# A fifth stack buffer, later loads of the read-out, and maxima's rows made by ScalarE and VectorE

## The chip, the cores and the metric

The kernel runs on one core of a Trainium2 chip. Five engines work side by side: TensorE (PE in the profile; its weight loads are PEld), VectorE (DVE), ScalarE (ACT), GpSimd (POOL) and SyncE (SP), which here only issues DMAs. The metric is the device time of one execution in microseconds (us), the median of several runs; less is better.

## The reference

It is one transformer block on 2048 rows of 512 columns in float32. A condition vector gives six modulation rows; the first half is attention with a memory, the second a feed-forward layer of 1792 columns. What this case touches is the attention: 32 heads of 16 columns, four segments of 512 rows, causal softmax within each segment, and a read-out of the memory of the segments before.

```python
for s in range(N):                       # N = 4 segments of L = 512 rows
    qs, ks, vs = q[:, :, s], k[:, :, s], v[:, :, s]
    logits = jnp.einsum("bhqd,bhkd->bhqk", qs, ks) * scale + mask
    p = _softmax(logits, axis=-1)
    a_dot = jnp.einsum("bhqk,bhkd->bhqd", p, vs)
    pq = phi(qs)
    num = jnp.einsum("bhld,bhde->bhle", pq, M)
    den = jnp.einsum("bhld,bhd->bhl", pq, z)[..., None] + 1e-6
    o = g * (num / den) + (1.0 - g) * a_dot
    outs.append(o)
    M = M + jnp.einsum("bhld,bhle->bhde", phi(ks), vs)
    z = z + jnp.einsum("bhld->bhd", phi(ks))
```

## The kernel before

**Stages.** First the projections q, k, v and the memory read-out for all segments (to about 195 us), then the attention loop (195 to 510), then the feed-forward layer. Every float32 matrix is split into a high and a low part, so that a product is three matmuls.

**Head groups.** The loop runs over 32 groups Q, each of four heads of one segment (Q // 8 is the segment). The split q and k of a group lie in DRAM (QD, KD) and are loaded into a pair of SBUF tiles, the stacks `qst` and `kst`: `load_stacks` (L175) issues four DMAs of 192 KB. There are four pairs of stacks (`NK`, L165); group Q uses pair Q % 4. `new_stack` (L168) allocates a pair and fills rows with ones by ScalarE.

**Two passes per group.** The S pass (`s_unit`, L616) multiplies q by k (matmul L625), and VectorE takes the causal maximum of each row with one instruction (`masked_max`, L613). The maxima (tile `nm`) are turned into two further rows of the q stack: `m_rows` (L634) splits them into high and low parts on POOL (a copy, L638, and a subtraction, L639) into a tile `nmr`; `m_put` (L642) transposes them by a matmul (L644) and ScalarE copies the result to `ms`; `m_send` (L651) sends `ms` by two small DMAs (L654) into rows 48 and 49 of the stack. The T pass (`t_unit`, L674) multiplies k by q with these 50 rows (L686), so that the maximum is subtracted within the product, ScalarE takes the exponential (L689), POOL zeroes what lies above the diagonal (L671), and `pv_part` (L705) multiplies by v (L714). The S pass of a group runs two groups ahead of its T pass (`LEAD`), and six PSUM banks named `att` are shared by both.

**Read-out.** Two groups make a unit U. `pv_out` and `pv_store` (L731) write the result to DRAM (TD); `pv_in` (L734) loads it back in another layout as `dn` (the denominators) and `opk`, and `am_in` (L743) the memory's part `amB`. `den` (L754) inverts `dn` on VectorE, `den_store` (L764) writes it to DRAM (RD, L765), `rb_in` (L767) loads it back broadcast over the columns (`rbB`), `mix` (L771) multiplies and adds on POOL, and the output projection (`wo_part`, L796) follows.

**What sets the order.** It is written out by hand. `ORDER` (L26) is the pattern of one group: S and T units and slots c0 to c19. The table `PRM` (L28) gives each step its slot: `ap(pos, f, ...)` (L912) puts step f of a group at slot pos, where 20 slots are one group; so `'stacks': -59` puts the loads of group Q at 20 Q - 59, slot c1 of the group Q - 3. The loop at L997 walks through the pattern and issues what stands at each slot. All DMAs of the loop go through SyncE's queue, which works in the order of the program and waits at a DMA whose source is not ready.

## Time and profile before

| | |
|---|---|
| median of 3 runs | 822.83 us (821.05 to 827.29) |
| profiled execution | 823.3 us, span 821.6 us |
| PE busy | 796.4 us (97%) |
| DVE busy | 561.7 us (68%) |
| ACT busy | 453.0 us (55%) |
| POOL busy | 278.0 us (34%) |
| mean granted TensorE clock | 0.946 |
| bytes moved by DMA | 156.25 MB, 190 GB/s on average |

A row of the profile names the engine, the line of the kernel, the operation and the tiles (out<-in, buffer numbers left out). Idle time stands in brackets with what ended it: `[1.58 <-DMA qst<-QD]` is an idle time of 1.58 us that ended when the load of a q stack landed. The granted clock is the share of TensorE's full clock that the chip allowed in a stretch. Matmul ends are modelled, so a busy PE need not be one that works at its peak.

### The profile page before, as it was taken

The numbers are of one execution on the slowest core, as the hardware profiler recorded it, in microseconds if no ns is written. First come the engines' busy times: TensorE is split into PE (matmuls) and PEld (weight loads), VectorE is DVE, ScalarE is ACT, GpSimd is POOL, SyncE is SP. The second block draws the span as 40 slices with busy tenths as digits, with TensorE's granted clock in tenths as the row PEclk, the third lists the DMA queues.
The fourth block names the chain that finished last, engine by engine and source line by source line (L and its number), as shares of the span: only waits on it lengthen the run. The fifth ranks groups of instructions, "written<-read, shape, count | busy, mean of one in ns | idle before, by whom it ended". The sixth has DMA issues, their size and how long they took to land.

```text
span 821.6 us, 14382 instructions
## 1 busy us (share of the span) xinstructions
PE 796.4 (97%) x4532; PEld 550.8 (67%) x4532; DVE 561.7 (68%) x1624; ACT 453.0 (55%) x882; POOL 278.0 (34%) x503
## 2 busy tenths in 40 slices
PE   9999999999999999999898989999999999999998
PEld 4887877866444445454454545778888888888887
DVE  6766684578967857687785879978758864533423
ACT  4544444536867756576575857676845336653221
POOL 2205252302567544465486746034100403210000
PEclk9999999999968757799897999999999999999999
DMA  9759655493665564576676785467675635545443
GB/s 342 265 218 324 240 205 211 139 380 74 164 175 141 146 165 114 165 202 171 175 194 149 217 237 164 150 222 257 203 243 171 205 128 161 173 146 163 147 147 116
DMA packets 96564, 156.25 MB, mean 190 GB/s; under 512 B 15332, under 2 KB 31076, under 8 KB 96488
## 3 DMA queue, kind: packets, MB, share of 16 engines
q1 hardware_dynamic: 95624, 153.76, 60.2%
q10 hardware_dynamic: 864, 1.57, 0.5%
q8 instruction: 36, 0.59, 0.3%
q14 instruction: 40, 0.33, 0.1%
HBM read 93.95 MB, written 60.83 MB: 188 GB/s over the span
## 4 chain that ended last, share of the span: by engine, by line
PE 81%; DMA 9%; DVE 3%; ACT 2%; POOL 2%; SPq 1%; issue 1%; ACTq 0%; DVEq 0%; POOLq 0%
PE bx L1062 8%; PE pv L714 8%; PE att L686 7%; PE bx L1332 5%; PE att L625 5%; PE q L318 5%; PE by L1332 5%; PE bv L1332 5%; PE bv L1062 4%; PE k L318 4%; PE v L469 4%; PE mm L802 3%; DMA qst<-QD 3%; DMA qst<-ms 3%; PE spare L1332 2%; PE by L1062 2%
## 5 line engine op out<-in xcount | busy, mean ns | idle before, releaser
L613 DVE CUSTOM_DVE_ANT_0 dump<-att,maskb 128x512 bf16<-128x512 f32 (+3 forms) x512 | 223.1, 487 | 69.5 <-PE att L625 42.2
L686 PE MATMUL att<-qst,kst 50*128 50x512 f32 (+3 forms) x512 | 140.1, 403 | 6.7 <-DMA qst<-ms 4.1
L625 PE MATMUL att<-kst,qst 48*128 48x512 f32 (+3 forms) x512 | 132.0, 376 | 8.7 <-DMA qst<-QD 6.6
L686 PEld LDWEIGHTS att<-qst,kst 50*128 50x128 f32 x512 | 87.0, 211 | 67.0 <-DVE nm L613 47.4
L625 PEld LDWEIGHTS att<-kst,qst 48*128 48x128 f32 x512 | 85.5, 212 | 29.1 <-ACT ptc L689 7.7
L689 ACT ACTIVATE pta<-att 128x512 f32<-128x512 f32 x128 | 69.5, 597 | 39.4 <-PE att L686 36.3
L689 ACT ACTIVATE ptb<-att 128x384 f32<-128x384 f32 x128 | 63.3, 496 | 38.8 <-PE att L625 32.7
L846 POOL TENSOR_TENSOR wb<-wa 128x256 f32<-128x256 f32 x24 | 20.8, 865 | 152.1 <-DVE hr L867 69.0
L689 ACT ACTIVATE ptc<-att 128x384 f32<-128x384 f32 x128 | 57.0, 492 | 0.3 <-PE att L686 0.2
L671 POOL TENSOR_SCALAR_AFFINE_SELECT pta<-pta 128x256 f32<-128x256 f32 x64 | 26.8, 419 | 84.8 <-ACT pta L689 84.8
L138 DVE TENSOR_TENSOR gl<-s,gh 128x512 fp32r<-128x512 f32 x34 | 24.0, 706 | 42.4 <-ACT gh L135 42.4
L671 POOL TENSOR_SCALAR_AFFINE_SELECT ptc<-ptc 128x256 f32<-128x256 f32 x128 | 51.7, 414 | 1.7 <-ACT ptc L689 0.3
L135 ACT ACTIVATE gh<-s 128x512 fp32r<-128x512 f32 x34 | 21.3, 628 | 47.1 <-PE spare L1332 17.4
L671 POOL TENSOR_SCALAR_AFFINE_SELECT ptb<-ptb 128x256 f32<-128x256 f32 x64 | 26.4, 412 | 51.4 <-ACT ptb L689 51.3
L1067 ACT ACTIVATE s<-s,b1t 128x512 f32<-128x512 f32 x42 | 30.3, 721 | 21.7 <-DVE s L1071 21.6
L613 DVE DVE_READ_ACCUMULATOR2_ANT nm<- 128x1 f32 x512 | 42.2, 82 | 0.0
L1071 DVE TENSOR_TENSOR s<-bv,s 128x512 f32<-128x512 f32 x28 | 19.2, 687 | 30.1 <-PE bv L1062 20.7
L714 PE MATMUL pv<-pta,V 128*32 128x512 f32 x208 | 35.1, 754 | 0.0
L504 POOL TENSOR_SCALAR qp<-qp 128x512 f32<-128x512 f32 x12 | 18.5, 1541 | 42.2 <-ACT qp L499 42.2
L714 PE MATMUL pv<-ptc,V 128*32 128x256 f32 (+1 forms) x416 | 30.8, 372 | 0.0
L138 DVE TENSOR_TENSOR w1ml<-s,w1mh 128x512 fp32r<-128x512 f32 x18 | 13.0, 720 | 21.5 <-ACT w1mh L135 21.5
L802 PE MATMUL mm<-woh,oh 128*128 128x512 f32 x52 | 26.8, 516 | 0.0
(372 smaller groups left out, 2073.3 us busy)
## 6 DMA issues: line engine op xcount, KB each, us to landing
GD<-s SPq DMA_DIRECT2D x56, 256.0 KB
s<-GD SPq DMA_DIRECT2D x52, 256.0 KB
kst<-KD SPq DMA_DIRECT2D x64, 192.0 KB
qst<-QD SPq DMA_DIRECT2D x64, 192.0 KB
QD<-q SPq DMA_DIRECT2D x16, 512.0 KB
KD<-k SPq DMA_DIRECT2D x16, 512.0 KB
TD<-ts SPq DMA_DIRECT2D x32, 256.0 KB
xt<-X2D SPq DMA_DIRECT2D x28, 256.0 KB
```

The source lines that it names most:

```text
L138: lo_eng.tensor_tensor(out=lo, in0=src, in1=hi.bitcast(F32), op=ALU.subtract)
L318: pe.matmul(ps, a[:, k, 128 * g:128 * g + 128], b[k], start=(k == 0 and i == 0), stop=(k == KB - 1 and i == 2))
L469: pe.matmul(ps, a[k][:, 128 * b:128 * b + 128], w[:, k, :], start=(k == 0 and i == 0), stop=(k == KB - 1 and i == 2))
L613: v.tensor_tensor_reduce(out=dump[n_dump[0] % 2][:, :n], in0=src, in1=maskb[:, 512 - n:], scale=-1.0, scalar=-4 * NEG, op0=ALU.add, op1=AL ...
L625: pe.matmul(ps[:, o:o + n], q[:, 128 * i:128 * i + 128], k[:, :n], start=True, stop=True)
L671: pool.affine_select(out=t, in_=t, pattern=pattern, compare_op=ALU.is_ge, fill=0.0, base=0, channel_multiplier=-1)
L686: pe.matmul(ps[:, o:o + n], k[:, 128 * j:128 * j + 128], q[:, 128 * j:], start=True, stop=True)
L689: act.activation(pt[:, h, :], ps[:, :m], AF.Exp, scale=0.25)
L714: pe.matmul(ps[32 * c:32 * c + 32, lo:hi], V[4 * s + j][:, VW * hd:VW * hd + 32], pt[:, c // 2, lo - o:hi - o], start=start, stop=stop)
L802: pe.matmul(ps, a[:, 128 * b:128 * b + 128], w[:, g, :], start=(g == 0 and i == 0), stop=(g == 3 and i == 2))
L1062: pe.matmul(ps, a[:, i, k, :], b[k], start=start and k == 0 and c == 0, stop=k == 1 and c == 2, skip_group_check=not start)
L1332: pe.matmul(ps, a[:, c], w[:, lo:hi], start=(f == 0 and i == 0), stop=(last and i == 2))
```

## The change

There are four edits, made together.

1. **Stacks.** A fifth pair of stacks is allocated at the start of group 0 in the pool `late`. Groups up to 11 use the pairs as before; from group 12 on each group uses the pair of the group five before it (`home`). The loads of groups 12 and up are issued at slot 20 Q - 67, which is c13 of the group Q - 4, instead of c1 of the group Q - 3.
2. **Read-out.** `pv_in` moves 10 slots back (`dnl` 21 to 31), `den_store` 7 slots (`rdl` 2 to 9), `rb_in` 2 slots (`rbl`). Units 11 and 13 (`quick`) and the last two (`end`) keep their slots.
3. **Maxima's rows.** The copy of `m_rows` goes from POOL to ScalarE; the subtraction becomes a step of its own, `m_low`, on VectorE two slots later.
4. **Tiles.** `nmr` has two buffers instead of four.

```diff
  'mrows': -20,
+ 'mlow': -18,
  'mput': [-12, -12],
- 'stacks': -59,
+ 'stacks': [-59, -67],
  'den': 95,
- 'dnl': 21,
- 'rbl': 16,
- 'rdl': 2,
+ 'dnl': 31,
+ 'rbl': 18,
+ 'rdl': 9,
...
-    NK = 4
+    def home(Q):
+        return Q % 4 if Q < 12 else (Q - 13) % 5 if Q % 5 != 2 else 4
...
-        nmr = [sb.tile([128, 128], F32R, name=f"nmr{i}", bufs=1) for i in range(4)]
+        nmr = [sb.tile([128, 128], F32R, name=f"nmr{i}", bufs=1) for i in range(2)]
...
         def m_rows(Q):
...
-            pool.tensor_copy(hl[:, :, 0], n)
-            pool.tensor_tensor(out=hl[:, :, 1], in0=n, in1=hl[:, :, 0].bitcast(F32), op=ALU.subtract)
+            act.activation(hl[:, :, 0], n, AF.Copy)
+            nss[Q] = n, hl, r
+
+        def m_low(Q):
+            n, hl, r = nss[Q]
+            v.tensor_tensor(out=hl[:, :, 1], in0=n, in1=hl[:, :, 0].bitcast(F32), op=ALU.subtract)
             nss[Q] = r
...
+        at(0, 0, lambda: new_stack(4, late[0]))
         for Q in range(2, 32):
-            ap(20 * Q + PRM["stacks"], load_stacks, Q)
+            ap(20 * Q + PRM["stacks"][Q > 11], load_stacks, Q)
...
             ap(20 * Q + PRM["mrows"], m_rows, Q)
+            ap(20 * Q + PRM["mlow"], m_low, Q)
...
-                ap(den_at + PRM["rdl"], den_store, U)
+                ap(den_at + p["rdl"], den_store, U)
```

What stands on SyncE's queue from the maxima's rows of group 16 (ms16) to those of group 17, before the change (names with their buffer numbers: kst3 and qst3 are the stacks of group 19, TD7, RD5 and so on belong to units 7 and 5):

```order
L654 DMA qst0_1703<-ms16_3808 2x8x128 x2
L769 DMA rbB5_3834<-RD5_3742 128x1x512
L811 DMA xb0_2_3836<-in_x 128x512
L737 DMA dn6_3838<-TD6_3588 128x1x32
L739 DMA opk6_3840<-TD6_3588 128x1x512
L746 DMA amB6_3842<-AMD1_2_111 128x512
L732 DMA TD7_3831<-ts14_3832 128x512
L828 DMA X2D0_121<-xb0_1_3593 128x512
L180 DMA kst3_1990<-KD2_1_98 48x1024 x2
L180 DMA qst3_1989<-QD2_1_82 48x1024 x2
L654 DMA qst1_1711<-ms17_3933 2x8x128 x2
```

The same place after it; group 19 now uses the stacks kst1 and qst1, and the line numbers are those of the changed kernel, a few higher:

```order
L661 DMA qst3_1985<-ms16_3808 2x8x128 x2
L818 DMA xb0_2_3834<-in_x 128x512
L183 DMA kst1_1712<-KD2_1_98 48x1024 x2
L183 DMA qst1_1711<-QD2_1_82 48x1024 x2
L776 DMA rbB5_3843<-RD5_3746 128x1x512
L739 DMA TD7_3831<-ts14_3832 128x512
L835 DMA X2D0_121<-xb0_1_3591 128x512
L744 DMA dn6_3894<-TD6_3588 128x1x32
L746 DMA opk6_3896<-TD6_3588 128x1x512
L753 DMA amB6_3898<-AMD1_2_111 128x512
L661 DMA qst4_2071<-ms17_3933 2x8x128 x2
```

It is the same set of transfers; the loads moved from right ahead of ms17 to behind ms16 and xb0_2, and dn, opk and amB from the middle to right ahead of ms17.

On ScalarE at the start of group 0, before the change, the exponentials of the T pass (pta, ptb, ptc) follow each other, with the copy of ms behind them:

```order
L689 ACTIVATE ptb_2072<-att_1915 128x384
L689 ACTIVATE ptb_2072<-att_1916 128x384
L689 ACTIVATE ptc_2093<-att_1913 128x384
L689 ACTIVATE ptc_2093<-att_1914 128x384
L129 ACTIVATE ms_2110<-att_1916 32x128
```

and after it:

```order
L696 ACTIVATE ptb_2068<-att_1911 128x384
L176 ACTIVATE kst_2072<-one 32x1024 x2
L641 ACTIVATE nmr_1905<-nm_1901 128x2x8
L696 ACTIVATE ptb_2068<-att_1912 128x384
L696 ACTIVATE ptc_2093<-att_1909 128x384
L696 ACTIVATE ptc_2093<-att_1910 128x384
L130 ACTIVATE ms_2110<-att_1912 32x128
```

The two fills of the fifth stack (kst_2072, in group 0 alone) and the copy into nmr (in every group) stand between the first and the second exponential of ptb. On VectorE, in the same group, the maxima before the change:

```order
L613 ISA dump_1920,nm_1902<-att_1914,maskb 128x384
L613 ISA nm_1902 128x1
L613 ISA dump_1919,nm_1902<-att_1917,maskb 128x384
L613 ISA nm_1902 128x1
L613 ISA dump_1920,nm_1902<-att_1912,maskb 128x256
```

and after it, with the subtraction between the maxima of the first and the second unit of 384 columns:

```order
L616 ISA dump_1916,nm_1902<-att_1910,maskb 128x384
L616 ISA nm_1902 128x1
L646 TENSOR_TENSOR nmr_1905<-nm_1901,nmr_1905 128x2x8
L616 ISA dump_1915,nm_1902<-att_1913,maskb 128x384
L616 ISA nm_1902 128x1
L616 ISA dump_1916,nm_1902<-att_1908,maskb 128x256
```

POOL loses both operations, and nothing else changes place on it.

## The prediction

> **What bounds the kernel now.** I read the page first, then the waits of TensorE in the attention loop, then the loop cut into stretches by granted clock, then the timeline of PE and of SyncE around each stall.

> ```profile
> span 821.6 us, 14382 instructions
> PE 796.4 (97%) x4532; PEld 550.8 (67%) x4532; DVE 561.7 (68%) x1624; ACT 453.0 (55%) x882; POOL 278.0 (34%) x503
> ```

> PE is busy for 97% of the span, so waits alone are worth at most 25 us. But the busy time is not all at one speed. The stretches below show, after their length, PE's busy time (with instructions), granted clock, DMA share and GB/s. The loop over the 32 head groups runs from about 195 to 510 us (first row); the others are the seven where the clock was low and, for comparison, two at full clock.

> ```profile
> 195.00:510.00 315.00, 296.13 (x2180) 0.86 0.63 169
> 232.00:247.00 15.00, 15.00 (x92) 0.54 0.60 159
> 260.00:277.00 17.00, 16.95 (x97) 0.50 0.53 133
> 290.00:317.00 27.00, 27.00 (x145) 0.51 0.51 130
> 335.00:346.00 11.00, 11.00 (x66) 0.54 0.41 109
> 346.00:372.00 26.00, 25.64 (x208) 1.00 0.80 212
> 376.00:379.00 3.00, 3.00 (x15) 0.50 0.76 195
> 398.00:403.00 5.00, 5.00 (x31) 0.50 0.47 135
> 403.00:430.00 27.00, 25.14 (x213) 1.00 0.58 158
> 434.00:445.00 11.00, 11.00 (x53) 0.54 0.47 118
> ```

> Seven times the clock falls to half. Ahead of each stands a stall of PE (the timeline; in brackets the idle time and what ended it):

> ```profile
> 231.83 0.59 PE L686 MATMUL att<-qst,kst 50*128 50x512 f32 x2 [0.99 <-DMA qst<-ms]
> 260.05 0.89 PE L686 MATMUL att<-qst,kst 50*128 50x512 f32 x2 [0.68 <-DMA qst<-ms]
> 289.13 0.47 PE L625 MATMUL att<-kst,qst 48*128 48x512 f32 x1 [1.58 <-DMA qst<-QD]
> 334.21 0.59 PE L686 MATMUL att<-qst,kst 50*128 50x512 f32 x2 [0.50 <-DMA qst<-ms]
> 375.03 0.47 PE L625 MATMUL att<-kst,qst 48*128 48x512 f32 x1 [1.63 <-DMA qst<-QD]
> 396.72 0.76 PE L625 MATMUL att<-kst,qst 48*128 48x512 f32 x1 [3.03 <-DMA qst<-QD]
> 433.92 0.48 PE L644 MATMUL att<-identr,nmr 128*128 128x128 f32 x1 [2.77 <-POOL nmr L639]
> ```

> The price of half clock: the same matmul (L644) stands once per group, and two distances between its starts show a group at half clock and one almost wholly at full:

> ```profile
> 265.83 0.48 PE L644 MATMUL att<-identr,nmr 128*128 128x128 f32 x1
> 276.96 0.33 PE L644 MATMUL att<-identr,nmr 128*128 128x128 f32 x1
> 284.00 0.33 PE L644 MATMUL att<-identr,nmr 128*128 128x128 f32 x1
> ```

> 11.13 us against 7.04: a group loses 4.09 us, 37% of what it takes at half clock. With time at half clock as (1 - clock)/0.5 x length, the seven stretches lose 5.1, 6.3, 9.8, 3.7, 1.1, 1.9 and 3.7 us, 31.6 in all; the seven stalls themselves are 11.2. So a stall costs some three times more by the clock that follows it than by itself: on average 1.6 + 4.5 = 6.1 us.

> **The change part by part.** The profiled execution took 823.3 us (span 821.6 and 1.7 around it), the median is 822.83; the sum starts from 823.3.

> *Loads of groups 13 and up.* Before, SyncE issues a group's loads at the slot after the last use of the buffer; with the fifth buffer right behind the pair of the maxima's rows (ms) of the slots before, 0.4 of a group earlier. The gain in time is read from SyncE's rows: the ms pair, and the loads that would now follow it.

> ```profile
> 277.61 1.29 SPq L654 DMA_DIRECT2D qst<-ms  x2
> 281.07 0.87 SPq L180 DMA_DIRECT2D kst<-KD  x2
> ...
> 361.12 1.28 SPq L654 DMA_DIRECT2D qst<-ms  x2
> 366.74 1.15 SPq L180 DMA_DIRECT2D kst<-KD  x2
> ...
> 381.41 1.28 SPq L654 DMA_DIRECT2D qst<-ms  x2
> 387.34 1.04 SPq L180 DMA_DIRECT2D kst<-KD  x2
> ```

> The first pair is of group 13's loads, then 21's and 23's. Group 13: 281.07 - 278.90 = 2.2 us earlier, against a stall of 1.58. For group 21 one issue (xb) stays between, for group 23 two (xb, xt2), each some 0.43 (half of 0.87): 366.74 - 362.40 - 0.43 = 3.9 against 1.63, and 387.34 - 382.69 - 0.86 = 3.8 against 3.03. All three stalls go, with 0.6, 2.3 and 0.8 us to spare: (1.58 + 9.8) + (1.63 + 1.1) + (3.03 + 1.9) = 19.0 us. The stall of 0.50 at 334.21 is of ms rows that stood behind such loads; now the loads stand behind the rows: 0.50 + 3.7 = 4.2. What comes late next on that queue is ms in every second group, because the read-out loads (dn, opk, am) now stand 8 slots ahead of it instead of 18; priced under the fresh stalls.

> *The store of the denominators (den_store), 7 slots later.* SyncE waits there for VectorE, with the loads behind it:

> ```profile
> SPq L765 <- DVE dn L757: 30.4, 13, 4.4
> ...
> 252.19 0.35 SPq L765 DMA_DIRECT2D RD<-dn  x1
> 252.64 1.26 SPq L180 DMA_DIRECT2D kst<-KD  x2
> ...
> 255.64 1.31 SPq L654 DMA_DIRECT2D qst<-ms  x2
> ```

> Here the loads left only after the store at 252.19, and the ms pair at 255.64 queued behind them until 260.05. Moved behind loads and TD, the store holds back neither; the loads leave about 2 us earlier and that stall goes: 0.68 + 6.3 = 7.0 us. What waits now behind the store is rb_in, 9 slots on instead of 14: at 7.04 us for 20 slots 3.2 us. Its user, the mix on POOL, comes 13 slots after rb_in (4.6 us) instead of 15.

> *Maxima's rows.* POOL loses two operations a group; ScalarE gets the copy, VectorE the subtraction. PE no longer waits for POOL's queue: 2.77 + 3.7 = 6.5 us at 433.92. POOL's other work is not waited for there, so nothing else is late. VectorE's slack is small, in the first five groups (PE, PEld, DVE, ACT, POOL busy):

> ```profile
> 195.00:231.00 36.00, 35.10 (x301) 18.34 (x299) 34.79 (x163) 30.99 (x71) 21.08 (x53) 1.00 0.64 156
> ...
> L757 DVE TENSOR_SCALAR dn<-dn,omg x16: 241/378/1192, 230.7 to 520.5; 128x32 f32<-128x32 f32 x16
> ...
> 224.66 0.89 ACT L689 ACTIVATE ptb<-att 128x384 f32<-128x384 f32 x2
> ...
> 225.09 0.56 DVE L613 CUSTOM_DVE_ANT_0 dump<-att,maskb 128x384 bf16<-128x384 f32 x1 [0.18 <-PE att L625]
> ```

> 1.21 us idle in 36, so 0.24 a group. No VectorE row shows this subtraction; the nearest is its small one on dn, 0.24 to 1.19 us; I take the least, nearest for a tile of 16 columns, which uses the slack up; at 1.19 each time the twelve groups below would lose 11 us more. It also waits for ScalarE's copy, which stands behind the first of the two ptb exponentials (done near 225.1) and takes as much as the small operations here, some 0.25: ready near 225.4, where the next maximum began at 225.09. So a group pays between 0 (VectorE late anyway) and 0.5 us; I take the middle, for the twelve groups where PE has no work of the output projection: 3 us (0 to 6). Later groups have slack. A gain from the copy itself is excluded, since both engines only get work.

> The spread of L757, 0.24 to 1.19 us, is the row to weigh. [...]

> *Ones of the fifth buffer.* Two ScalarE operations at the start of group 0:

> ```profile
> L173 ACT ACTIVATE kst<-one x8: 1053/1056/1060, 155.6 to 187.2; 32x1024 fp32r<-32x1024 f32 x8
> ```

> 2.1 us in front of exponentials, with ScalarE idle for 5.0 of 36 us there: PE feels between 0 and 2.1; I take 1. Half as many nmr buffers: each is read by L644 well before it is written again two groups later; nothing.

> *pv_in 10 slots later.* den now follows it after 13 slots, 4.6 us in a full-clock group. The nearest rows are the landings of two other read-out loads in the chain of waits (start, us):

> ```profile
> 280.40 6.36 DMA opk<-TD
> ...
> 405.70 4.53 DMA rbB<-RD
> ```

> They took 4.5 and 6.4 us, so VectorE may wait for dn from 0 to 1.8 us. It was in no such wait before.

> *Fresh stalls.* With the low clock gone the same bytes must move in less time: the DMA share is 0.80 in the full-clock stretch from 346 against 0.41 to 0.60 in the four long low ones. I count two stalls with a fall of the clock that are new (by dn, or ms behind dn, opk and am): 2 x 6.1 = 12.2 us, with 0 to 4 as bounds. The one at 231.83 stays: its rows stand behind loads at the old place.

> Smaller ms waits that cost no clock (the longest 1.1) bring 1.1.

> ```profile
> PE att L686 <- DMA qst<-ms: 4.1, 7, 1.1
> ```

> Sum: 823.3 - 19.0 - 4.2 - 7.0 - 6.5 - 1.1 + 3 + 1 + 12.2 = **801.7 us**, say 802. Without fresh stalls 789.5; with four, 814.

> **Rivals.** One per cent, about what a measurement here can tell, is 8.2 us: faster means under 814.6, slower over 831.1.

> *The queue takes it back.* At full clock the DMA queue is as late as before, at other transfers: ms behind the read-out loads in every second group, S behind rb and TD. Six fresh stalls: 789.5 + 36.6 = 826. For it: the share of 0.80 at full clock leaves little room for bursts. Against: the loads' spare times above, and that in the groups between nothing big stands ahead of ms. Chance 0.14.

> *The clock does not follow the stalls.* If the low stretches have another cause, only idle time is won: 11.2 - 0.99 + 1.1 = 11.3, less 4 of costs: 816. For it: 1.86 us of idle in 403 to 430 (25.14 busy of 27) brought no fall. Against: all seven falls begin within 2 us of a stall. [...] Chance 0.10, on both sides of 814.6.

> *Slower: VectorE becomes the bound and the clock stays low.* The subtraction waits for ScalarE, the maxima slip, PE idles some tenths in each group, and half clock, once entered at the ones of group 0, is not left. Each such group costs 4.09 us; ten more than in the 789.5 case (which has one, at 232) make it slower than 831, thirteen give 843. For it: DVE busy for 34.79 of 36 us. Against: the idle pieces of 403 to 430 at clock 1.00. Chance 0.12.

> *Better than forecast:* no fresh stall and the one at 231.83 gone too (its loads can leave before opk): 789.5 - 6.1 = 783. Chance 0.08.

> **Numbers.** The forecast case, 789 to 814, has 0.56. Faster: 0.56 + 0.08 + 0.05 = 0.69; same: 0.14 + 0.05 = 0.19; slower 0.12. The range runs from 781 to 826: it leaves out the slow case, part of the queue's and little below.

> **What would show it.** Right: no PE wait on QD in groups 13 to 31 above 0.5 us; none on nmr; SyncE's wait for dn at L765 shrunk; fewer than four low-clock stretches, loop near 294 us. Wrong: PE waits on ms in every second group, VectorE waiting for dn or for ScalarE's copy by some tenths per group, low clock between 195 and 230.

## The result

The changed kernel takes **837.73 us** (median of 20 runs, 826.8 to 850.7) against 824.19 us for the kernel before on the same chip (20 runs, 816.1 to 830.0). The ratio is 1.0125, 95% interval 1.0088 to 1.0162: slower by 1.25%. I had forecast 802 us, and 826 at most. Ratios here leave disturbed executions out, so that they need not equal the quotient of the medians; where the two differ in sign, or the interval takes in 1, I call a run undecided.

The profiled execution took 848.3 us, in the upper part of the runs; a second profile of the same kernel, taken later, has a span of 834.1. The head of its page:

```profile
span 846.6 us, 14379 instructions
PE 814.0 (96%) x4532; PEld 556.7 (66%) x4532; DVE 568.1 (67%) x1654; ACT 459.5 (54%) x916; POOL 266.9 (32%) x439
```

The loop as a whole, and three stretches that were at half clock from end to end (length, PE's busy time with instructions, granted clock, DMA share, GB/s):

```profile
195.00:534.00 339.00, 313.52 (x2183) 0.80 0.60 157
200.80:221.30 20.50, 20.50 (x106) 0.50 0.40 94
238.30:269.00 30.70, 30.70 (x181) 0.50 0.49 132
282.70:313.40 30.70, 30.70 (x176) 0.50 0.46 117
```

The mean clock of the loop is 0.80 where it was 0.86, and three stretches alone hold 81.9 us at half clock; all seven of before held 88.7. In all there are eleven, 133.1 us. At the start of each stands a stall of PE again, but none of them is one of those that I counted on removing. The timeline of PE, in brackets what ended the idle time:

```profile
199.61 0.33 PE L651 MATMUL att<-identr,nmr 128*128 128x128 f32 x1 [1.11 <-ACT ptb L696]
236.94 0.30 PE L651 MATMUL att<-identr,nmr 128*128 128x128 f32 x1 [0.51 <-DVE nmr L646]
282.64 0.89 PE L693 MATMUL att<-qst,kst 50*128 50x512 f32 x2 [1.42 <-DMA qst<-ms]
327.43 0.89 PE L693 MATMUL att<-qst,kst 50*128 50x512 f32 x2 [3.11 <-DMA qst<-ms]
...
514.82 1.08 PE L693 MATMUL att<-qst,kst 50*128 50x512 f32 x3 [3.17 <-DMA qst<-ms]
```

The first is the wait behind ScalarE's fill of the fifth stack, the second the wait for VectorE's new subtraction, and all nine others are waits for the maxima's rows (ms), 21.5 us together. TensorE's waits and SyncE's longest waits in the loop (us in total, times, longest):

```profile
PE att L693 <- DMA qst<-ms: 22.6, 10, 3.5
PE att L651 <- ACT ptb L696: 1.1, 1, 1.1
PE att L693 <- DVE nm L616: 0.8, 2, 0.6
PE att L651 <- DVE nmr L646: 0.5, 1, 0.5
...
SPq L661 <- ACT ms L130: 96.0, 29, 7.0
SPq L183 <- PE att L693: 12.1, 8, 2.7
...
SPq L772 <- DVE dn L764: 3.9, 2, 2.3
```

The waits for loads (qst<-QD) and for POOL are gone, and SyncE's wait for the denominators (dn) fell from 32.6 us over the same stretch to 3.9. The waits for ms grew from 4.1 to 22.6 us.

**An account of the loop.** From each trace three numbers can be read: the length of the loop (first S matmul to last matmul on the stacks), the time in it in which PE runs no matmul, and the time at half clock. What lies outside the loop is 488 to 491 us in every kernel below but one (499.6 in the run with short stores).

| us | loop | PE idle | at half clock | stretches |
|---|---|---|---|---|
| before | 333.1 | 18.9 | 88.7 | 7 |
| after | 356.8 | 25.5 | 133.1 | 11 |
| after, second profile | 344.4 | 22.6 | 102.4 | 9 |

Over all 20 profiles of this study, a fit by least squares gives: loop = 285.1 + 0.91 x idle + 0.37 x time at half clock, with no profile off by more than 2.7 us. So of the 23.7 us between the two profiles 6.0 are idle time (0.91 x 6.6) and 16.4 are clock (0.37 x 44.4). The two profiles of the changed kernel differ by 12.4 us in the loop, and the same formula gives 14.0 for that: the spread between executions of one kernel is mostly clock, too.

### The profile page after: what moved, and what is told of

The parts are those of the page before. It is cut to its first block, busy times and chain, and to the rows that moved or that the text cites. A ratio compares the mean times of both kernels' runs of the same rounds, so it can differ in the third digit from the quotient of the medians.

```text
span 846.6 us, 14379 instructions
## 1 busy us (share of the span) xinstructions
PE 814.0 (96%) x4532; PEld 556.7 (66%) x4532; DVE 568.1 (67%) x1654; ACT 459.5 (54%) x916; POOL 266.9 (32%) x439
## 4 chain that ended last, share of the span: by engine, by line
PE 78%; DMA 11%; DVE 4%; ACT 3%; SPq 2%; issue 2%; POOL 0%; ACTq 0%; DVEq 0%
PE pv L721 9%; PE att L693 8%; PE bx L1071 8%; DMA qst<-ms 6%; PE att L628 5%; PE q L321 5%; PE bx L1341 5%; PE k L321 4%; PE bv L1071 4%; PE by L1341 4%; PE bv L1341 4%; PE v L472 4%; PE mm L809 3%; PE spare L1341 2%; PE mm L721 2%; PE by L1071 2%
## 5 line engine op out<-in xcount | busy, mean ns | idle before, releaser
L693 PE MATMUL att<-qst,kst 50*128 50x512 f32 (+3 forms) x512 | 147.2, 426 | 23.6 <-DMA qst<-ms 22.6
L693 PEld LDWEIGHTS att<-qst,kst 50*128 50x128 f32 x512 | 92.9, 228 | 88.0 <-DVE nm L616 36.7
L628 PE MATMUL att<-kst,qst 48*128 48x512 f32 (+3 forms) x512 | 138.2, 393 | 0.3 <-ACT ptb L696 0.2
L628 PEld LDWEIGHTS att<-kst,qst 48*128 48x128 f32 x512 | 91.4, 226 | 21.0 <-ACT ptc L696 9.6
L1076 ACT ACTIVATE s<-s,b1t 128x512 f32<-128x512 f32 x42 | 30.3, 721 | 21.5 <-DVE s L1080 21.5
L721 PE MATMUL pv<-pta,V 128*32 128x512 f32 x208 | 39.0, 833 | 0.0
L721 PE MATMUL pv<-ptc,V 128*32 128x256 f32 (+1 forms) x416 | 30.4, 369 | 0.0
L721 PE MATMUL pv<-ptb,V 128*32 128x384 f32 x208 | 28.0, 618 | 0.0
```

What stands on the lines that cost most here:

```text
L628: pe.matmul(ps[:, o:o + n], q[:, 128 * i:128 * i + 128], k[:, :n], start=True, stop=True)
L693: pe.matmul(ps[:, o:o + n], k[:, 128 * j:128 * j + 128], q[:, 128 * j:], start=True, stop=True)
L721: pe.matmul(ps[32 * c:32 * c + 32, lo:hi], V[4 * s + j][:, VW * hd:VW * hd + 32], pt[:, c // 2, lo - o:hi - o], start=start, stop=stop)
L1076: act.activation(dst, src, AF.Gelu_apprx_tanh, bias=b1t[:, f:f + 1])
```

## The experiments

All ran with the kernel before beside them on the same chip. The chips differ between the groups of runs, so that runs of different groups are compared by what each took over the kernel before beside it. "rows" and "loads" are TensorE's waits in the loop for the maxima's rows (qst<-ms, at the T matmul) and for stack loads (qst<-QD), from the profile of that run; "half" is the time at half clock.

| run | median us | before there | ratio (95%) | rows | loads | half |
|---|---|---|---|---|---|---|
| e1 read-out back | 839.80 | 826.76 | 1.0188 (1.0049 to 1.0327) | 10.7 | 2.4 | 109.2 |
| e2 read-out loads back | 850.28 | 826.76 | 1.0272 (1.0101 to 1.0442) | 22.9 | 0 | 136.5 |
| e3 ones by GpSimd | 831.05 | 826.76 | 1.0136 (1.0039 to 1.0233) | 23.9 | 0 | 95.6 |
| e4 maxima by GpSimd | 833.87 | 826.76 | 1.0127 (0.9998 to 1.0256) | 14.6 | 0 | 122.9 |
| e5 = e3, stack loads back | 839.65 | 825.84 | 1.0194 (1.0144 to 1.0243) | 22.3 | 2.9 | 102.4 |
| e6 stacks alone | 835.09 | 825.84 | 1.0083 (1.0035 to 1.0131) | 12.1 | 2.9 | 95.6 |
| e7 read-out alone | 838.56 | 825.84 | 1.0174 (1.0114 to 1.0235) | 27.4 | 0 | 81.9 |
| e8 maxima alone | 821.06 | 825.84 | 1.0033 (0.9975 to 1.0091) | 4.5 | 4.9 | 61.4 |
| e9 = e3, rows by ScalarE's queue | 859.00 | 826.01 | 1.0371 (1.0316 to 1.0425) | 23.1 | 0 | 102.4 |
| e10 before, rows by ScalarE's queue | 868.54 | 826.01 | 1.0496 (1.0434 to 1.0558) | 39.4 | 0 | 126.3 |
| e11 store alone | 827.81 | 826.01 | 0.9981 (0.9940 to 1.0023) | 10.3 | 2.9 | 105.8 |
| e12 read-out loads alone | 834.78 | 826.01 | 1.0131 (1.0090 to 1.0173) | 14.0 | 0.4 | 92.2 |
| e13 = e3 without later K loads | 813.83 | 827.11 | 0.9961 (0.9906 to 1.0016) | 9.2 | 0 | 64.9 |
| e14 before, short stores | 899.88 | 827.11 | 1.0958 (1.0907 to 1.1010) | 30.2 | 21.0 | 174.1 |
| e15 = e3, read-out back | 828.28 | 827.11 | 1.0054 (1.0009 to 1.0098) | 9.8 | 5.7 | 71.7 |
| e17 changed kernel again | 838.10 | 827.11 | 1.0174 (1.0071 to 1.0277) | 13.6 | 0 | 102.4 |
| e18 = e15, rows earlier | 827.18 | 824.68 | 1.0043 (1.0007 to 1.0080) | 9.1 | 1.0 | 88.7 |
| e19 = e8, rows earlier | 819.00 | 824.68 | 0.9909 (0.9870 to 0.9948) | 4.1 | 8.2 | 92.2 |

### First: one part of the change taken back

The theory was that the read-out loads, now right ahead of the rows, make these late (theory Q in the expectations); its rivals were VectorE's subtraction (V) and the fill at group 0 (S).

e1, the whole read-out back:

```diff
- 'dnl': 31,
- 'rbl': 18,
- 'rdl': 9,
+ 'dnl': 21,
+ 'rbl': 16,
+ 'rdl': 2,
```

> The changed kernel with the slots of pv_in, den_store and rb_in as before the change; stacks, maxima's rows and nmr stay changed. Theory Q (the read-out loads dn, opk and am, now right ahead of the maxima's rows on SyncE's queue, make those rows late): PE's waits for ms fall from 22.6 us to 6 or less and the time to 810 to 820. Theory V (VectorE's subtraction, waiting for ScalarE and for POOL's operations, is the cost): ms waits may fall, the time stays at 832 or above. Theory S (the two fills of ones at the start of group 0 put the clock into its low state for the first groups): 832 or above too, with low clock from 200 to 222 us.

e2, only the read-out loads (dn, opk, am) back:

```diff
- 'dnl': 31,
+ 'dnl': 21,
```

> The changed kernel with pv_in alone back at its slot (dnl 21); den_store and rb_in stay late. Theory Q in its narrow form (pv_in is the step that matters): as with all three back or better, 808 to 820, ms waits 6 us or less, and SyncE still hardly waits for dn. If den_store or rb_in are to blame instead: ms waits stay near 20 us and the time at 830 or above. V and S: 832 or above.

e3, the ones of the fifth stack by GpSimd:

```diff
-            act.activation(kst[i][r:r + 32].rearrange("p e n -> p (e n)").bitcast(F32R), one[r:r + 32].to_broadcast([32, 1024]), AF.Copy)
+            dst, src = kst[i][r:r + 32].rearrange("p e n -> p (e n)").bitcast(F32R), one[r:r + 32].to_broadcast([32, 1024])
+            if i == 4:
+                pool.tensor_copy(dst, src)
+            else:
+                act.activation(dst, src, AF.Copy)
```

> The changed kernel with the ones of the fifth stack filled by POOL instead of ScalarE, all else changed. Theory S: no low clock before 230 us, VectorE's 2.15 us wait for the copy in group 0 gone, time 5 to 9 us less (829 to 833). Theory Q: ms waits stay at about 20 us, time at 830 to 838. If the fills cost only themselves (1 to 2 us): 836.

e4, the maxima's rows by GpSimd as before (`m_low` and its slot go):

```diff
-            act.activation(hl[:, :, 0], n, AF.Copy)
...
+            pool.tensor_copy(hl[:, :, 0], n)
+            pool.tensor_tensor(out=hl[:, :, 1], in0=n, in1=hl[:, :, 0].bitcast(F32), op=ALU.subtract)
```

> The changed kernel with the maxima's rows made on POOL again, all else changed. Theory V: VectorE's 7.1 us of waits for ScalarE's copy and PE's 16.6 us behind the subtraction go, time 822 to 828. Theory Q: ms waits stay near 20 us or grow, since the rows come no earlier; time 832 to 845, with PE waiting for POOL's nmr again by 3 us or more.

Theory Q in this narrow form fell: with only the read-out loads back (e2) the waits for the rows were as long as ever, 22.9 us, and the time rose to 850.28. With the whole read-out back (e1) they halved to 10.7, but the time, 839.80, did not follow. e4 is undecided. The trace of e3 answered clearly: the stretch that was at half clock in the changed kernel is at full clock there. First the fills in the changed kernel and the exponential behind them, for which PE waited, then the stretch in e3:

```profile
196.83 2.12 ACT L176 ACTIVATE kst<-one 32x1024 fp32r<-32x1024 f32 x2
...
199.08 0.47 ACT L696 ACTIVATE ptb<-att 128x384 f32<-128x384 f32 x1
```

```profile
200.80:221.30 20.50, 20.50 (x185) 1.00 0.67 169
```

In the same 20.5 us PE ran 185 instructions instead of 106. A single stall of 1.11 us, from two instructions that run once, cost 0.37 x 20.5 = 7.6 us in that execution; the second profile (e17) shows 10.2 us at half clock in that place, so 3.8. All five profiles with ScalarE's fill have such a stretch, from 199.0 to 200.8 us on and 10.2 or 20.5 us long; none of the other fifteen has half clock between 195 and 219 us. What the fill costs in time is less sharp. Two pairs of runs differ in it alone. By the medians it costs 6.7 us between e17 and e3 (838.10 less 827.11, against 831.05 less 826.76) and 11.9 between e1 and e15 (13.0 and 1.2 over the kernel before); by the ratios 0.4 and 1.3%, and the first result (1.0125) is no slower than e3 (1.0136). The intervals are as wide as these differences.

### Second: one part of the change alone

> The changed kernel with the ones of its fifth pair written by GpSimd, and with the loads of all groups at the old slot, 59 ahead of their group; the fifth pair stays in use, and so do the late read-out and the split maxima. Theory P (the place): a load 67 ahead of its group leaves right behind the maxima's rows of the group that is due next, and these rows are what lands late. Then TensorE's waits for these rows fall from the 23.9 us that the same kernel with the loads at 67 showed to under 8 us, and the time from 831 to 815 to 822 us. Theory F (the fall of the clock, wherever it starts): any stall halves the clock, the stretches of low clock stay near 95 us in sum whichever wait they start from, and the time stays within 4 us of 831.

> The kernel before with the fifth pair of stacks (its ones written by GpSimd, not ScalarE) and the loads 67 ahead from the thirteenth group on; read-out and maxima as before, but two buffers for the rows of maxima in place of four. Theory P: the waits for the loads go, as I forecast (19.0 us of the sum), but waits for the maxima's rows of 10 us or more come in their place, and the time is within 1% of the kernel before. My forecast's terms: no wait for a load, waits for the rows of maxima at most the 4.1 us of before, and 19 us less than the kernel before.

> The kernel before with only the three numbers of the read-out changed (read-out loads 10 slots later, the store of the denominators 7 slots later and their spreading 2 slots plus). My forecast's term: SP's wait for the denominators falls from 30.4 us to under 6, and the time by 5 to 9 us. Theory Q2: the read-out loads, issued later, fall together with the maxima's rows or the stack loads; then the waits for loads or rows grow by what the other wait gave, and the time is within 0.5% of before or longer.

> The kernel before with only the maxima split as in the change: the copy by ScalarE, the remainder by VectorE two slots later, two buffers for the rows. My forecast's terms: the waits for GpSimd at the turning of the maxima go (8.1 us in all before), VectorE gets 3 us more work; 3 to 8 us less than before. Theory V2: ScalarE's copy and VectorE's remainder are late as often as GpSimd was, so the waits at the turning stay at 6 us or more, and the time is within 0.5% of before or longer.

e5 is e3 with `'stacks': [-59, -59]`. e6 is the kernel before with `home`, the fifth pair (ones by GpSimd), `'stacks': [-59, -67]` and two buffers for nmr. The edits of e7 and e8 are these:

```diff
- 'dnl': 21,
- 'rbl': 16,
- 'rdl': 2,
+ 'dnl': 31,
+ 'rbl': 18,
+ 'rdl': 9,
```

```diff
+ 'mlow': -18,
...
-            pool.tensor_copy(hl[:, :, 0], n)
-            pool.tensor_tensor(out=hl[:, :, 1], in0=n, in1=hl[:, :, 0].bitcast(F32), op=ALU.subtract)
+            act.activation(hl[:, :, 0], n, AF.Copy)
...
+            v.tensor_tensor(out=hl[:, :, 1], in0=n, in1=hl[:, :, 0].bitcast(F32), op=ALU.subtract)
```

Theory P (the loads' new place makes the rows late) fell with e5: at the old place the rows waited 22.3 us, hardly less than in e3, and over the kernel before e5 lost 9.5 us more than e3 by the medians, 0.6% by the ratios. So beside the late read-out the earlier loads seem to help (the intervals overlap), while beside the old read-out (e6) they cost 0.8%; the parts do not add. The read-out alone (e7) is slower by 1.7%, with the longest waits for rows of these four and the waits for loads gone:

```profile
PE att L686 <- DMA qst<-ms: 27.4, 9, 5.8
PE att L644 <- POOL nmr L639: 2.8, 1, 2.8
...
SPq L765 <- DVE dn L757: 2.9, 3, 1.7
```

SyncE's wait for dn shrank as I had forecast (2.9 us here, 32.6 over the same stretch in the kernel before), but the time rose all the same. The maxima alone (e8) are undecided, by their median 4.8 us faster.

### Third: the two halves of the read-out, and another queue

> The changed kernel with the ones of the fifth pair written by GpSimd, and with the maxima's rows issued by ScalarE's DMA queue instead of SP's; every other transfer as in the change. Theory L (the line behind the read-out and the loads): in the trace of the run with the read-out alone the rows that are late stand right behind a 256 KB read-out load and four stack loads in SP's queue and take 3.5 to 6.7 us to land, the others 1.9 us. If it is their place in that queue, they land from a queue of their own in about 2 to 3 us, TensorE's waits for them fall from 23.9 us to under 6, and the time from 831 to 805 to 816 us (ScalarE pays about 1 us a group for issuing, where it has slack). Theory E (the 16 DMA engines themselves are backed up): the rows share these engines with the same transfers from whichever queue, the waits stay at 15 us or more, and the time is 828 us or more.

> The kernel before, with the maxima's rows issued by ScalarE's queue. TensorE's waits for the rows are only 4.1 us there, but SP stands 66.4 us waiting for ScalarE's copy of the rows in front of them, and the loads behind. Theory L: SP no longer stands there, loads leave earlier, the 6.6 us of waits for loads shrink too; 3 to 12 us less than before. Theory E: as before within 0.5%, or longer by what ScalarE pays (up to 8 us).

> The kernel before with only the store of the denominators 7 slots later and its spreading 2 slots later (the read-out loads stay at the old slot). My forecast's term: SP's wait for the denominators falls from 32.6 us to under 8, and 3 to 8 us less than before. Theory L: the spreading load, two slots further back, then leaves behind the rows as before, so the rows are no later: waits for them under 8 us. If the waits for the rows grow to 15 us or more, the store and the spreading are to blame for the slower read-out.

> The kernel before with only the read-out loads 10 slots later. Theory L: the 256 KB load then leaves 8 slots ahead of the rows of every second group and right behind the stack loads, and these rows wait in line: TensorE's waits for the rows 18 us or more (4.1 before), 8 to 16 us slower than before. If the waits stay under 8 us, it takes the later store as well (which lets SP run ahead), or the store alone.

```diff
-                sp.dma_start(qst[home(Q)][64 * h + 48:64 * h + 50], ms[16 * h:16 * h + 16])
+                act.dma_start(qst[home(Q)][64 * h + 48:64 * h + 50], ms[16 * h:16 * h + 16])
```

is the edit of e9 (on e3) and, with the old index of the stacks, of e10 (on the kernel before). e11 sets `'rbl': 18` and `'rdl': 9` in the kernel before, e12 `'dnl': 31`.

The store alone is undecided (0.9981; its interval ends at 0.9940, which is 5 us, so the 7.0 of the forecast lie outside). The read-out loads alone cost 1.3%: in the kernel before these are the half to blame, though in the changed kernel taking them back alone (e2) did not help. SyncE's timeline in e12 shows why, and the chain of waits what became of the second ms transfer issued there:

```profile
359.52 0.64 SPq L737 DMA_DIRECT2D dn<-TD  x1
360.25 0.58 SPq L739 DMA_DIRECT2D opk<-TD  x1
360.87 0.46 SPq L746 DMA_DIRECT2D amB<-AMD  x1
361.43 1.76 SPq L654 DMA_DIRECT2D qst<-ms  x2
```

```profile
339.98 5.12 DMA qst<-ms
...
362.54 5.51 DMA qst<-ms
```

8 KB take 5.5 us to land when opk and amB (256 KB each) were issued in the 2.3 us ahead of them, and four stack loads shortly before. It is not the place in SyncE's queue, though. From ScalarE's queue the rows were as late: in e9 they waited 23.1 us, in e10, where nothing of the change is in, 39.4. In e9's chain a transfer of rows from ScalarE's queue, with SyncE's timeline beside it:

```profile
472.05 6.38 DMA qst<-ms
```

```profile
471.19 0.89 SPq L187 DMA_DIRECT2D kst<-KD  x2
472.13 1.37 SPq L187 DMA_DIRECT2D qst<-QD  x2
```

The rows landed 6.4 us after they were issued, beside four stack loads of the other queue. e10 is the clearer of the two: SyncE no longer waited for ScalarE's copy in front of the rows (66.4 us in the kernel before), no load was late any more, and the kernel lost 5%; I read it that the loads now left together with the rows. That ScalarE now has the issues to do as well is not where the time went: TensorE's waits for ScalarE are 0.5 us in e9 and 0.9 in e10, though those for VectorE's maxima grew to 7.1 and 3.7.

### Fourth: bytes, and the number of pieces

> The changed kernel with the ones by GpSimd, and without the loads of K from the seventeenth group on (old K stays in the stacks): 384 of the 768 KB that a group loads, about a quarter of all bytes that move per group, are left out, so the output is not the reference's. Theory E (the DMA engines are backed up and the small rows of maxima wait behind what is already in them): behind group 17 (some 330 us on) TensorE's waits for the rows fall to under 2 us in all, against about 16 us there in the same kernel with the loads, low clock there under 20 us, and the time to 800 to 815 us from 831. Theory N (the rows are late by their own chain: maxima, turning, ScalarE's copy, two issues): the waits stay at 8 us or more, and the time within 8 us of 831.

> The kernel before with the store of the attention output in four pieces of 17 of 32 rows, as only those are read again: 120 KB a group less (a twelfth of the loop's bytes), three issues a group more on SP (some 1.2 us a group, where SP stands still for about 3 us a group). Theory E: waits for rows and loads (10.7 us before) shrink to 5 us or less and the time by 4 to 10 us. If the number of transfers counts and not their bytes, it is 5 us or more slower than before.

> The changed kernel with the read-out at its old slots and the ones of the fifth pair by GpSimd: what is left of the change are the fifth pair with its earlier loads and the split maxima. If the read-out and ScalarE's fill are all of the loss, it takes the 819 us that the sum of my terms gives with the fresh stalls at the two or three that its trace shows, at most 826. If the earlier loads are themselves a loss (as the run with the stacks alone showed, at 835), 830 to 838 us, with waits for the rows of 8 us or more.

> The changed kernel once more, beside the run with its ones by GpSimd (831.05 on another chip) and beside the run here without the read-out. If ScalarE's fill at group 0 costs what the low clock behind it does (20.5 us at half clock, some 7 us), this is 836 to 841 us, and again low from about 200 to 220 us in its trace.

```diff
         for st, dd in ((kst[home(Q)], KD), (qst[home(Q)], QD)):
+            if Q > 16 and st is kst[home(Q)]:
+                continue
```

(e13, on e3), and

```diff
-            sp.dma_start(TD[Q // 2][Q % 2], tss.pop(Q))
+            t = tss.pop(Q)
+            for c in range(4):
+                sp.dma_start(TD[Q // 2][Q % 2, 32 * c:32 * c + 17], t[32 * c:32 * c + 17])
```

(e14, on the kernel before). e13 leaves out the K loads of the later groups, so that its output is not the reference's. e15 is e3 with the read-out of e1; e17 is the changed kernel itself.

With the later K loads gone, the time fell by 17.6 us against e3 by the medians over the kernel before, by 1.75% by the ratios. TensorE's waits for the rows between 330 and 500 us, first in e3, then in e13:

```profile
PE att L697 <- DMA qst<-ms: 18.1, 7, 4.0
```

```profile
PE att L699 <- DMA qst<-ms: 6.4, 2, 3.2
```

And that stretch (length, busy, clock, DMA share, GB/s), again e3 ahead of e13:

```profile
330.00:500.00 170.00, 149.80 (x1065) 0.85 0.63 167
```

```profile
330.00:500.00 170.00, 159.69 (x1227) 0.96 0.56 159
```

That speaks for theory E: the rows wait for other transfers in the DMA engines, and fewer bytes give the wait back. Two waits of 3.2 us stayed, where I had expected under 2 in all. At the first of them the rows left at 418.87, again right behind the read-out loads, with SyncE's timeline:

```profile
417.00 0.64 SPq L750 DMA_DIRECT2D dn<-TD  x1
417.68 0.59 SPq L752 DMA_DIRECT2D opk<-TD  x1
418.31 0.46 SPq L759 DMA_DIRECT2D amB<-AMD  x1
418.87 1.38 SPq L667 DMA_DIRECT2D qst<-ms  x2
```

But bytes are not the whole of it. e14 moves 120 KB a group less and is almost 10% slower. Its chain of waits holds pieces of the store and the rows in turn:

```profile
327.75 7.25 DMA TD<-ts
335.01 4.96 DMA qst<-ms
353.03 7.33 DMA TD<-ts
360.38 4.28 DMA qst<-ms
374.28 9.19 DMA TD<-ts
```

Each line of TD is one piece of a store, 17 rows or 34 KB, the second or third of its four, and it lands 7.3 to 9.2 us after it was issued. The pieces of one store land one behind the other, 1.1 to 1.9 us apart, the last 8.3 to 11.1 us after the first was issued. The whole store of the kernel before, all 128 rows, took 4.9 us (median). An estimate to set beside this: the stretch from 346 us of the kernel before moved 212 GB/s at a share of 0.80 of the 16 engines, so one engine at work moved 212 / 0.80 / 16 = 16.6 GB/s on average, and at that rate the four pieces (139,264 bytes) would take 8.4 us one behind the other. So the pieces were about as slow as one engine would be by this estimate; which engines carried them no trace here shows. That the engines need not be full for a transfer to be late, a stretch of the changed kernel shows, in which an ms transfer was on its way. The chain of waits, and the stretch:

```profile
403.50 5.62 DMA qst<-ms
```

```profile
403.50:409.10 5.60, 3.33 (x25) 0.99 0.75 226
404.00:407.00 3.00, 2.83 (x17) 1.00 0.55 193
```

For 3 us the sixteen engines are little more than half busy on average (share 0.55) while the rows wait. The trace also keeps every DMA packet. From 404.3 to 407.2 us 8.7 packets are in flight on average, where from 403.0 to 403.8 us there are 16.8 and from 407.4 to 409.0 us 15.4; the 32 packets of the rows (512 bytes each) start only from 407.59 to 407.99 us, two in flight at a time for the most part. The landings on the semaphores differ as well, in both kernels: 16 for each stack load, amB and whole store, 9 for each opk, dn and rbB, 3 for each transfer of rows; what a landing stands for was not shown. So the rows waited while about half as many packets were in flight as before and after. What held them back in that stretch was not shown.

It is not the only way in which the rows are late. At the nine waits of the changed kernel with a fall of the clock, the rows' first packet came 24.0 us in all beyond the 1.25 us that it takes at the least; for 13.8 of these at most ten packets were in flight, for the rest the engines were fuller.

e15 and e17 divide up the loss. Without the late read-out and without the fill, what is left (fifth pair, earlier loads, split maxima) is 828.28 against 827.11: ratio 1.0054. The changed kernel beside it is at 838.10. Of its 11.0 us there, some 7 are the fill, some 3 the read-out and 1 the rest by the medians; by the ratios the read-out and the fill change places (0.8 and 0.4%). With intervals of 0.4 to 1.0% to either side this division is rough. Either way e15 falls short of the 819 at which it would have borne out my terms, though its waits for rows and loads together are back near those of before (15.5 against 10.7).

### Fifth: a faster version

> The run with fifth pair and split maxima but the old read-out (828.28 us), and two shifts: the turning of the maxima and the sending of the rows one slot (0.35 us) earlier, and GpSimd's low part of the output weights three slots later, so that it begins behind VectorE's subtraction. Subtraction 0.17 to 0.2 us in every one of the groups 5 to 8 instead of 1.29; no wait of 0.5 us at the turning there; waits for the rows from 9.8 us to about 7. If falls of the clock follow these short waits, two or three stretches of low clock go and the time falls by 4 to 10 us, to 818 to 824; if the DMA engines set the pace, the waits move to the loads and it stays within 4 us.

> The run with the split maxima alone (821.06 us) and the same two shifts. The three waits of 0.5 us and the one of 0.3 at the turning go, the waits for the rows (4.5 us there) shrink by a third of a us each, to about 2; those for the loads (4.9) stay. 812 to 819 us, which would be 1 to 2% less than the kernel before; if the pace is set by the DMA engines, 819 to 824.

```diff
- 'mput': [-12, -12],
+ 'mput': [-13, -12],
...
- 'wl': [32, 66, 77, 81],
+ 'wl': [32, 66, 77, 84],
```

The reason for the second line is the subtraction. Its durations in the changed kernel (ns: least, median, most):

```profile
L646 DVE TENSOR_TENSOR nmr<-nm,nmr x32: 167/176/1291, 189.2 to 517.3; 128x16 fp32r<-128x16 f32 x32
```

The timeline of VectorE and POOL ahead of the stall at 236.94:

```profile
235.51 1.29 DVE L646 TENSOR_TENSOR nmr<-nm,nmr 128x16 fp32r<-128x16 f32 x1 [0.27 <-ACT nmr L641]
...
235.49 1.27 POOL L910 TENSOR_TENSOR wol<-wor,woh 128x512 fp32r<-128x512 f32 x1
```

The subtraction began 0.02 us behind GpSimd's and ended 0.03 us behind it, after seven times its median. Six of the 32 took 0.97 us or more. The two lines did not cure it: in e19 two stalls of 0.5 us for the subtraction remain, since GpSimd's operation, three slots later, still began 0.01 and 0.07 us ahead of it there. So these runs do not tell what the cure is worth. e18 was as e15. e19, the split maxima alone with rows one slot earlier, is **faster than the kernel before by 0.9%** (0.9909, 0.9870 to 0.9948) and faster than the changed kernel by about 2%. Its one profile, span 823.8, shows no fewer waits than before; the gain is in the 10 runs, not in a row that I can point to.

## Why the prediction was wrong

- **What goes, went.** The waits for loads in groups 13, 21 and 23 and the wait for POOL at 433.92 are gone, and SyncE's wait for the denominators shrank from 32.6 to 3.9 us. They were 19.0, 6.5 and 7.0 us of the sum. What each was worth in time no run shows by itself, but the store's 7.0 was too much: alone (e11) it is worth 5 us at most, since the waits for loads fell from 6.6 to 2.9 us and those for rows rose from 4.1 to 10.3. The stacks alone (e6) took away waits for loads (2.9 left) and brought waits for rows (12.1) in the same way.
- **The step that failed is the term of the fresh stalls.** I named the place, ms in every second group behind dn, opk and am, but counted two stalls with 0 to 4 as bounds. There were nine falls of the clock behind waits for ms. The nine cost 0.91 x 21.5 + 0.37 x 81.9 = 49.9 us, 5.5 each where I had 6.1. That the price came out is luck in part: the stalls were longer (2.4 us against 1.6), the half clock behind each shorter (9.1 us against 12.7). Nine instead of two is 37.7 us, as much as all the gains of the sum together. My rival "the queue takes it back" was the mechanism, with six stalls and a chance of 0.14, and the first sign that I had named for being wrong, waits on ms in every second group, is what groups 17 to 25 show.
- **Why nine.** I held against that rival that nothing big stands ahead of ms in the groups between, and looked at the order of SyncE's queue. e9 and e10 show that the order of a queue is not all that the rows wait for: sent from another queue they were as late. What is still on its way in the DMA engines when they leave delays them; e13 shows it by taking bytes away (18.1 us of waits fell to 6.4), and at 404.3 to 407.2 us the rows waited with 8.7 packets in flight on average, about half of the 15 to 17 around that stretch.
- **The ones of the fifth buffer** were priced at 1 us (0 to 2.1) as idle time. The idle time was 1.11, inside the bounds; the fall of the clock behind it was left out, which I had charged to every other stall. It cost 7.6 and 3.8 us in the two profiles; by the runs it is somewhere between nothing and 12 us.
- **The subtraction** (3 us, 0 to 6). I had taken 0.24 us; it took 0.17 to 0.25 in 26 of 32 groups, and 0.98 to 1.29 in the other six. In each of these six a TENSOR_TENSOR of GpSimd (L910 four times, L798 twice) had begun before it, and the subtraction ended 0.03 us behind that one. In that execution one such stall, 0.51 us, stood ahead of 30.7 us at half clock, 11 us, as much as I had put on 1.19 us in each of twelve groups. e19 shows that the split of the maxima as a whole is no loss where the rows are sent a slot earlier; alone (e8) it is undecided.
- **The rival "the clock does not follow the stalls"** fell: the clock accounts for 16.4 of the 23.7 us between the profiles.
- **The slower rival** had the right sign with the low clock from the ones of group 0 on. (Its ten groups give 789.5 + 40.9 = 830.4, so it would have taken eleven to pass 831.) But VectorE did not become the bound (TensorE's waits for its maxima are 0.8 us in the loop), and the clock came back at 221.3.

Check of the sum: 789.5 (all stalls but that at 231.83 gone) less 6.1 for that one, which went as well, plus 49.9 for the nine, 7.6 for the clock behind the fill and 11.4 for that behind the subtraction is 852 us; the profiled execution took 848.3. The terms of the changed kernel are read from this same execution, so this shows that they leave nothing large out, not that they would forecast another one.

## What to carry to other kernels

A small transfer that TensorE waits for was here as late as the large ones on their way when it left (5.5 us in e12 and 6.4 in e9, against 1.9 at the least in the changed kernel), whichever queue it was sent from: before you move a load, list what is in flight at each small urgent transfer, not only what stands ahead of it in its queue. Price every new wait of TensorE, also of an instruction that runs once, with the clock that falls behind it: here a wait of 0.51 us stood ahead of 30.7 us at half clock, 11 us. And a fix that speeds up a loop may meet the DMA next: in the kernel before the DMA share was 0.80 in the full-clock stretch from 346 us and 0.41 to 0.60 in the four long ones at half clock. Count the bytes per group at the speed you hope for.

## What the runs showed that I had not expected

| idle in a piece of 3.413 us, us | clock stays | clock falls |
|---|---|---|
| under 0.01 | 823 | 0 |
| 0.01 to 0.6 | 177 | 7 |
| 0.6 to 1.4 | 54 | 65 |
| over 1.4 | 0 | 109 |

With 0.6 to 1.4 us of idle time in one piece the clock fell in 65 of 119 cases, and with more it always did (taken on to the end of each loop, one piece with 1.48 us did not). Where a stall lies in this grid may count as well, and I take that to be why runs of one kernel spread over 2 to 3%; no run here shows it by itself. All 178 returns to full clock followed a piece without any idle time, but most such pieces did not bring one; what decides that stays open.

**More queues made it worse.** Sending the rows from ScalarE cost 5% in the kernel before (e10), and in e9 the loss is 2.3% larger than in e3 by the ratios. It seems that SyncE's waiting in front of the rows had kept the loads out of their way.

**A store of fewer bytes took longer.** 136 KB in four pieces of 17 rows took 8.3 to 11.1 us from the first issue to the last landing where 256 KB in one piece took 4.9 (median), and the kernel became almost 10% slower.
